# A planned one-core kernel: a table step moved between engines, the PE fillers redistributed, four rows of the combination in four banks

## The chip, the cores and the metric

One core of a Trainium2 chip runs the whole program. The metric is the device time of one execution in microseconds; seven executions of the kernel before have a median of 192.67 us, from 191.19 to 193.7. The profiled execution of the kernel before took 193.35 us, and its trace spans 191.2 us from the first to the last instruction.

The engines carry these names in the profile: PE is the matrix engine (PEld its weight loads), DVE the vector engine, ACT the scalar engine, POOL the GpSimd engine, SP the engine that here only issues transfers. Results of PE go to PSUM, which has eight banks; everything else is in SBUF.

## The reference

Sequence length S is 2048, width D 448, MLP width F 1792, all in bf16. The steps that matter:

```
kv  = (causal 4-tap filter of k with shift_k) * v
y   = irfft(rfft(kv, 2S) * rfft(ssm_k, 2S))[:S] + kv * ssm_D        # a long convolution along S
h   = x + layernorm(x) * y                                          # A_q is x
n   = layernorm(layernorm(h))                                       # the MLP's own norm on top of B's input norm
h2  = h + transpose( gelu( n^T . w1 + b1 ) . w2 + b2 )              # contraction over S, then over F
```

The MLP contracts over the sequence: w1 is 2048 x 1792 and w2 is 1792 x 2048.

## The kernel before

The sequence is split into 16 rows (index r) of 128 positions. A row is a tile of 128 partitions x 448 columns. The convolution is done as a two-stage Fourier transform with matmuls, and the names of the stages are:

- **Tables.** `emit_tables` makes the table `E` of sines (32 matrices of 128 x 128) in two halves, h = 0 for rows 0 to 7 and h = 1 for rows 8 to 15. A half goes through an integer product (L751), an addition (L756), an AND (L759, always DVE) and two sines on ACT (L764). In the kernel before, L751 and L756 of half 0 run on DVE and those of half 1 on POOL. Small index tables follow: counters on POOL, a few fields on DVE up to L745, then L771, L775 and L788 on POOL, which make the second-stage matrix `FW` and the inverse ones.
- **Filler matmuls.** `dummy` (L904) and `emit_warm` (L1047) issue matmuls whose results nobody reads. `N_W0` stand at the start, `N_WK` after each of three groups of transposes of the filter ssm_k, `N_WZ` between the last inverse matmul and the last stage of the convolution, `N_WI` inside that last stage.
- **kT.** `emit_kT` transposes ssm_k with 64 small matmuls (L914) in eight groups of one PSUM bank each; each group is copied out once (L652 on ACT or L655 on DVE, the lines of the helper `evac`).
- **kv.** `emit_kv` first spreads the four taps over the partitions with four matmuls (L868), each copied out as one tap; then, for 8 pairs of rows, two products on DVE (L879), eight matmuls that add them (L885), and one product with v on DVE (L888).
- **k1 and u1.** `emit_stage1` is the first Fourier stage, for the filter (k1) and for kv (u1): per row two matmuls (L933) into a pair of banks, one copy on ACT (L943) into one of eight ring buffers, and two transfers that shuffle partitions (L947), one on POOL's queue and one on SP's. A ring buffer is free again when its two transfers have landed.
- **k2 and u2.** `emit_stage2` (L964) is the second stage, 16 evacuations each (k2 with a scale: L653 on ACT, L656 on DVE; u2: L652, L655). `emit_ct` transposes `E` into `ET`: POOL gathers columns of `E` into four chunks (L985, L990), PE transposes them (L996), one evacuation per chunk.
- **i1.** `emit_products_i1` multiplies the spectra on DVE (L1015), does the first inverse stage on PE (L1027), evacuates, and shuffles with 32 transfers (L1037).
- **i2, the combination.** `emit_i2` runs over rows: two matmuls (L1103), the gate on ACT (L1110), the combination with x on DVE (L1117), a sum of squares on ACT (L1133), four to five tiny steps on POOL (L1140 to L1152, the last a power), and the normed row `Q` on DVE (L1158). Rows 0 and 1 use other statistics (L1123, L1125) and no ACT step. Statistics of x itself come earlier (L1069, L1071 on DVE; L1074, L1077 on POOL). In the kernel before, the two matmuls of any row from 2 on wait for the gate of the row before it.
- **MLP.** `emit_mlp` runs the first seven column groups of w1 row by row as the rows of `Q` come (L1198, 7 matmuls a row into seven banks), the other seven with `Q` complete (L1208), then the second layer (L1218, 224 matmuls) and the sum with h (L1222), whose rows go out as they are done.

The order on each engine is not written by hand. `_Sched` records every operation with a due time (`sch.t0`, set from the constants T_...), an estimated duration (`est`, or a formula in `est_of`), what it reads and writes, and which PSUM bank or ring buffer it needs. `schedule` then plays the operations through on estimated times: at each moment a free engine takes the ready operation with the earliest due time. Operations with `engs=FX` go to ACT or DVE, whichever the plan finds free. What comes out is one fixed list for each engine; on the chip each engine works its list strictly in that order and waits at semaphores. So a changed constant or estimate can move any instruction.

Of the kernel before, what the change touches and what calls it, by code (L numbers as in the profile page):

```python
# [7 lines left out]
ALU = mybir.AluOpType  # L8
# [501 lines left out]
def _build(nc, A_q, A_k, A_v, A_shift_k, A_ssm_k, A_ssm_D, B_w1, B_b1, B_w2, B_b2, out):  # L510
# [55 lines left out]
    with ctx:  # L566
# [72 lines left out]
        T_KV, T_DKV, T_KT, T_K1, T_DK1, T_U1, T_DU1 = -37.75, 0.96, -43.81, -39.56, 0.55, 0.0, 0.9  # L639
        T_K2, T_U2, T_D2, T_CT, T_BIAS, T_I1, T_DI1 = 29.29, 9.62, 1.375, 22.37, 56.3, 12.82, 0.974  # L640
        T_Q, T_DQ, T_I2, T_DI2, T_M1, T_W1 = 83.98, 17.938, 85.76, 0.401, 91.84, 122.45

        T_TH, T_TN = -38.0, -30.0
        T_CP, T_XL, T_WB = 20.0, -37.92, 154.44
        N_WZ, N_WI, N_W0, N_WK = 24, 16, 9, 5
# [15 lines left out]
        def emit_tables():  # L661
# [85 lines left out]
            for h in range(2):  # L747
# [3 lines left out]
                op(("dve", "pool")[h], lambda e, W, h=h, ph=ph: e.tensor_tensor(  # L751
# [4 lines left out]
                op(("dve", "pool")[h], lambda e, W, ph=ph: e.tensor_scalar(  # L756
# [331 lines left out]
        def emit_i2():  # L1088
# [4 lines left out]
            for g, (r0, ng) in enumerate(GR):  # L1093
                oh = o_hst + 64 * g
                hs = view(oh, [16], f32)
                for i in range(ng):
# [5 lines left out]
                    for h in range(2):  # L1102
                        k = op("pe", lambda e, W, b=b, r=r, h=h: e.matmul(  # L1103
                            Pb(b), ET[:, 2 * r + h, :], TZ[:, r, h, :], start=(h == 0), stop=(h == 1)),
                           r=[r_ET(r)] + tz, bw=[b], n=D, after=av[-1:] if r >= 2 and h == 0 else ())
# [8 lines left out]
                    av.append(op(FX, gate, r=[(o_qst + 16 * r, 16), (o_c2, 16)], w=tz, br=[b], n=D, kind="psum"))  # L1114
# [6 lines left out]
                    if ng == 1:  # L1121
                        op("dve", comb, r=rx, w=tz, n=D, est=690.0)
                        op("dve", lambda e, W, hs=hs, A=A: e.bn_stats(out=hs[:, 8:14], in_=A),  # L1123
                           r=tz, w=[(oh + 32, 24)], n=D, kind="1x")
                        op("dve", lambda e, W, hs=hs: e.bn_aggr(out=hs[:, 0:2], in_=hs[:, 8:14]), r=[(oh + 32, 24)],  # L1125
                           w=[(oh, 8)], n=6)
                        mv = [(oh, 4), (oh + 4, 4)]
                        mean, var, rst = hs[:, 0:1], hs[:, 1:2], hs[:, 2:3]
                        o_r = oh + 8
                    else:  # L1130
                        op("dve", lambda e, W, hs=hs, i=i, comb=comb: comb(e, W, acc=hs[:, i:i + 1]), r=rx,
                           w=tz + [(oh + 4 * i, 4)], n=D, est=750.0)
                        op("act", lambda e, W, hs=hs, A=A, i=i: e.activation(out=JK, in_=A, func=ACT.Square,  # L1133
                                                                             scale=1.0 / math.sqrt(D),
                                                                             accum_out=hs[:, 2 + i:3 + i]),
                           r=tz, w=[(oh + 8 + 4 * i, 4), (o_JK, DB)], n=D, est=790.0)
                if ng == 2:
# [4 lines left out]
                       r=[(oh, 8)], w=[(oh + 16, 8)], n=2)  # L1142
                    op("pool", lambda e, W, hs=hs: e.tensor_tensor(out=hs[:, 6:8], in0=hs[:, 4:6], in1=hs[:, 4:6],
                                                                   op=ALU.mult), r=[(oh + 16, 8)], w=[(oh + 24, 8)], n=2)
                    op("pool", lambda e, W, hs=hs: e.tensor_tensor(out=hs[:, 8:10], in0=hs[:, 2:4], in1=hs[:, 6:8],
                                                                   op=ALU.subtract),
                       r=[(oh + 8, 8), (oh + 24, 8)], w=[(oh + 32, 8)], n=2)
# [3 lines left out]
                   r=mv[1:], w=mv[1:], n=2)  # L1151
                op("pool", lambda e, W, var=var, rst=rst, ng=ng: e.tensor_tensor(out=rst, in0=var, in1=cst[:, 0:ng],  # L1152
                                                                                 op=ALU.pow),
                   est=750.0, r=mv[1:] + [(o_c2, 16)], w=[(o_r, 4 * ng)], n=2)
                for i in range(ng):
# [5 lines left out]
                       r=[(o_TZ + r * 2 * DB, 2 * DB), mv[0], (o_r, 4 * ng)], w=[(o_Q + r * DB, DB)], n=D, kind="4x")  # L1161
                if g == 2:
                    emit_warm(N_WI, T_I2 + 0.5, lambda: i2_last[1:2])
# [114 lines left out]
```

## Time and profile before

| what | value |
|---|---|
| profiled execution, time / span | 193.35 us / 191.2 us |
| median of the seven executions | 192.67 us |
| PE busy / DVE / ACT / POOL | 176.6 / 109.9 / 97.5 / 76.9 us |
| first copy of k1 (L943) starts | 14.72 us |
| last product with v (L888) ends | 50.49 us |
| last spectrum product (L1015) ends | 82.17 us |
| last shuffle before the combination lands | 90.21 us |
| first MLP matmul (L1198) starts | 98.14 us |
| MLP without interleaved combination rows starts | 115.45 us |
| last matmul ends | 188.29 us |

Starts and ends are read from the timeline (start, duration, engine, line) and from the chain that ended last. The chain is followed back from the last instruction: at each step to what released it, or to the instruction before it on its engine. PE's busy time holds the fillers too, so a busy PE alone does not say that PE does useful work.

### The profile page before, as it was taken

What the parts mean: (1) busy time and instruction counts of PE and PEld (TensorE: products, weight loads), DVE (VectorE), ACT (ScalarE), POOL (GpSimd) and SP (SyncE); (2) the same over time, 40 slices, a digit from 0 to 9 for tenths busy, and PEclk for the clock granted to TensorE, in tenths of its full rate; (3) what the DMA queues carried; (4) which work ended last, traced back from release to release, by engine and by line L of the source; (5) the groups of instructions that cost most, each with busy time, mean ns of one, the idle gap of its engine ahead of it and who ended that gap; (6) DMA issues with size and microseconds to landing.
All of it is one profiled execution on the core that took longest, in us unless ns stands there. A gap on an engine that the chain in (4) does not pass through costs nothing.

```text
span 191.2 us, 2820 instructions
## 1 busy us (share of the span) xinstructions
PE 176.6 (92%) x1031; PEld 92.3 (48%) x1031; DVE 109.9 (57%) x176; ACT 97.5 (51%) x142; POOL 76.9 (40%) x180
## 2 busy tenths in 40 slices
PE   7949999899988899895989999999999999999993
PEld 2813444234443333242334445555556777777772
DVE  8885679988799999996668975100000222122221
ACT  3477799987989899960489855171221000000000
POOL 8966688679770044468238876000000000000000
PEclk9996699999999999999699999999999999999999
DMA  5997458887539999753899999000000011111111
GB/s 167 418 418 271 143 171 216 233 228 226 173 114 314 393 358 362 233 161 109 282 421 418 418 403 364 8 0 0 0 0 3 8 40 48 48 51 48 48 48 48
DMA packets 15724, 35.43 MB, mean 185 GB/s; under 512 B 3869, under 2 KB 9886, under 8 KB 15710
## 3 DMA queue, kind: packets, MB, share of 16 engines
q1 hardware_dynamic: 11102, 25.59, 35.7%
q0 software_dynamic: 4608, 9.66, 17.0%
q8 instruction: 8, 0.13, 0.3%
q14 instruction: 6, 0.05, 0.1%
HBM read 22.37 MB, written 1.84 MB: 127 GB/s over the span
## 4 chain that ended last, share of the span: by engine, by line
PE 67%; ACT 11%; POOL 7%; DVE 7%; DMA 5%; issue 1%; POOLq 0%
PE ps L1218 22%; PE ps L1208 11%; PE ps L1198 10%; DMA arena<-arena 5%; ACT arena L652 5%; PE ps L1103 4%; PE ps L933 4%; PE ps L1027 4%; PE ps L885 4%; PE ps L964 3%; ACT arena L653 2%; POOL arena L947 2%; ACT arena L1110 2%; POOL arena L756 2%; PE ps L1047 2%
## 5 line engine op out<-in xcount | busy, mean ns | idle before, releaser
L1222 DVE SCALAR_TENSOR_TENSOR arena<-ps,arena 128x448 bf16<-128x448 f32 x16 | 10.9, 684 | 57.9 <-PE ps L1218 57.9
L1218 PE MATMUL ps<-arena 128*128 128x448 bf16 x224 | 42.5, 352 | 0.0
L1218 PEld LDWEIGHTS ps<-arena 128*128 128x128 bf16 x224 | 32.3, 144 | 10.1
L943 ACT CAST arena<-ps 128x896 bf16<-128x896 f32 x32 | 26.9, 926 | 2.5 <-PE ps L933 2.0
L947 POOL DMA_DIRECT2D arena<-arena x32 | 19.3, 603 | 10.3 <-ACT arena L943 7.0
L652 ACT CAST arena<-ps 128x896 bf16<-128x896 f32 (+1 forms) x27 | 22.1, 931 | 1.9 <-PE ps L964 1.1
L1198 PE MATMUL ps<-arena 128*128 128x448 bf16 x112 | 23.0, 352 | 0.0
L1208 PE MATMUL ps<-arena 128*128 128x448 bf16 x112 | 21.4, 352 | 0.0
L933 PE MATMUL ps<-arena 128*128 128x448 bf16 x64 | 17.5, 390 | 3.4 <-ACT arena L652 2.5
L1188 ACT ACTIVATE arena<-ps,arena 128x448 bf16<-128x448 f32 x14 | 8.2, 640 | 20.7 <-PE ps L1208 14.7
L1110 ACT ACTIVATE arena<-ps,arena 128x448 f32<-128x448 f32 x16 | 11.5, 724 | 13.1 <-PE ps L1103 10.7
L879 DVE TENSOR_TENSOR arena<-arena 128x1792 bf16<-128x1792 bf16 x16 | 17.5, 1130 | 0.0
L1037 POOL DMA_DIRECT2D arena<-arena x16 | 9.4, 591 | 19.4 <-DVE arena L655 10.8
L964 PE MATMUL ps<-arena 128*64 128x448 bf16 x128 | 16.0, 360 | 1.0 <-DVE arena L655 0.4
L1015 DVE TENSOR_TENSOR arena<-arena 128x1792 bf16<-128x1792 bf16 x16 | 16.5, 1085 | 0.2 <-ACT arena L653 0.2
L1198 PEld LDWEIGHTS ps<-arena 128*128 128x128 bf16 x112 | 11.0, 98 | 10.2
L1208 PEld LDWEIGHTS ps<-arena 128*128 128x128 bf16 x112 | 11.0, 98 | 10.2
L1027 PE MATMUL ps<-arena 64*128 64x448 bf16 x128 | 14.0, 352 | 1.9 <-ACT arena L652 1.1
L1117 DVE SCALAR_TENSOR_TENSOR arena<-arena 128x448 f32<-128x448 bf16 x16 | 10.8, 685 | 8.0 <-ACT arena L1110 8.0
L885 PE MATMUL ps<-arena 128*128 128x448 bf16 x64 | 14.5, 354 | 0.6 <-ACT arena L943 0.5
L1103 PE MATMUL ps<-arena 128*128 128x448 bf16 x32 | 9.2, 376 | 3.0 <-DMA arena<-arena 2.3
L933 PEld LDWEIGHTS ps<-arena 128*128 128x128 f16 x64 | 5.8, 106 | 12.6 <-ACT arena L652 3.0
(88 smaller groups left out, 205.9 us busy)
## 6 DMA issues: line engine op xcount, KB each, us to landing
arena<-arena POOLq DMA_DIRECT2D x48, 196.0 KB, 4.7
arena<-in_B_w_dram SPq DMA_DIRECT2D x8, 896.0 KB, 14.2
arena<-in_B_w_dram SPq DMA_DIRECT2D x2, 2048.0 KB, 9.9
arena<-in_B_w_dram SPq DMA_DIRECT2D x2, 1536.0 KB, 18.0
arena<-in_A_k_dram SPq DMA_DIRECT2D x4, 448.0 KB, 7.3
arena<-in_A_v_dram SPq DMA_DIRECT2D x4, 448.0 KB, 7.9
arena<-in_A_q_dram SPq DMA_DIRECT2D x4, 448.0 KB, 4.6
out_dram<-arena SPq DMA_DIRECT2D x7, 224.0 KB, 1.9
```

Of the source, the lines that this page charges most:

```text
L652: return e.copy(out=dst(), in_=src())
L879: op("dve", lambda e, W, T=T, i=i, r=r: e.tensor_tensor(out=T[:, i], in0=KH[:, r:r + 4, :], in1=WT, op=ALU.mult), r=[(o_KH + r * DB, 4 * D ...
L885: op("pe", lambda e, W, b=b, T=T, i=i, j=j: e.matmul(Pb(b, i), ID, T[:, i, j, :], start=(j == 0), stop=(j == 3)), r=[(o_ID, 256), (o + (i ...
L933: op("pe", lambda e, W, b=b, r=r, h=h, dl=dl: e.matmul(Pb(b, h), E[:, 2 * r + h, :], src[:, r, :], start=True, stop=not dl), r=[r_E(r), (o ...
L943: return e.copy(out=dst, in_=Ppair(b)) if W == "act" else e.tensor_copy(out=dst, in_=Ppair(b))
L947: shuf[tag + q_ + str(r)] = shuf[tag + q_] = op(q_, lambda e, W, w=w, p0=p0, a=a, b_=b_, j0=j0: e.dma_start(T[p0:p0 + 29:4, j0:j0 + (b_ - ...
L964: op("pe", lambda e, W, b=bs[h], h=h, j=j, c=c, par=par: e.matmul(PS[64 * par:64 * par + 64, b.slots[c], 0:D], FW[:, 64 * c:64 * c + 64], ...
L1027: k = op("pe", lambda e, W, b=bs[h], m=ms[h], par=par, t=t, tab=tab, xy=xy, P=P: e.matmul(Pb(b, par), tab[P, :], MR(m.slots[0])[P, xy, :], ...
L1103: k = op("pe", lambda e, W, b=b, r=r, h=h: e.matmul(Pb(b), ET[:, 2 * r + h, :], TZ[:, r, h, :], start=(h == 0), stop=(h == 1)), r=[r_ET(r) ...
L1198: op("pe", lambda e, W, r=r, fc=fc, b=bs[fc]: e.matmul(Pb(b), W1A[:, r, 128 * fc:128 * fc + 128], Q[:, r, :], start=(r == 0), stop=(r == R ...
L1208: op("pe", lambda e, W, r=r, fc=fc, b=b: e.matmul(Pb(b), W1B[:, r, 128 * (fc - n0):128 * (fc - n0) + 128], Q[:, r, :], start=(r == 0), sto ...
L1218: op("pe", lambda e, W, r=r, fc=fc, b=b: e.matmul(Pb(b), W2[fc // 7][:, fc % 7, r:S:R], G[:, fc, :], start=(fc == 0), stop=(fc == NFC - 1) ...
```

## The change

The diff does five things. Line numbers stay as they are, since each hunk replaces as many lines as it removes.

1. L751 and L756 of table half 1 go from POOL to DVE.
2. Fillers: `N_WK` from 5 to 3 (after each of three transpose groups), `N_WZ` from 24 to 34 (before the combination), `N_WI` from 16 to 6 (inside it; they now follow row 3 instead of row 1).
3. In the combination, the matmuls of rows 0 to 3 wait for no gate; rows 4 and 5 wait for the gates of rows 1 and 2, and only rows from 6 on wait for the row before.
4. Due times of the transposes, k1, u1, u2, i1, the x loads, the statistics of x and the MLP change.
5. Estimates for the combination's operations change (gate 720/620, combination 690, square 570, power 700, other POOL steps 220, norm 510 ns).

```diff
-        T_KV, T_DKV, T_KT, T_K1, T_DK1, T_U1, T_DU1 = -37.75, 0.96, -43.81, -39.56, 0.55, 0.0, 0.9
-        T_K2, T_U2, T_D2, T_CT, T_BIAS, T_I1, T_DI1 = 29.29, 9.62, 1.375, 22.37, 56.3, 12.82, 0.974
-        T_Q, T_DQ, T_I2, T_DI2, T_M1, T_W1 = 83.98, 17.938, 85.76, 0.401, 91.84, 122.45
-        T_TH, T_TN = -38.0, -30.0
-        T_CP, T_XL, T_WB = 20.0, -37.92, 154.44
-        N_WZ, N_WI, N_W0, N_WK = 24, 16, 9, 5
+        T_KV, T_DKV, T_KT, T_K1, T_DK1, T_U1, T_DU1 = -37.75, 0.96, -26.42, -39.56, 0.44, 2.72, 0.9
+        T_K2, T_U2, T_D2, T_CT, T_BIAS, T_I1, T_DI1 = 29.29, -14.6, 1.375, 22.37, 56.3, 7.01, 0.974
+        T_Q, T_DQ, T_I2, T_DI2, T_M1, T_W1 = 83.98, 14.35, 85.76, 0.401, 102.98, 122.45
+        T_TH, T_TN = -36.0, -30.0
+        T_CP, T_XL, T_WB = 20.0, -35.53, 154.44
+        N_WZ, N_WI, N_W0, N_WK = 34, 6, 9, 3
...
-                op(("dve", "pool")[h], lambda e, W, h=h, ph=ph: e.tensor_tensor(
+                op("dve", lambda e, W, h=h, ph=ph: e.tensor_tensor(
...
-                op(("dve", "pool")[h], lambda e, W, ph=ph: e.tensor_scalar(
+                op("dve", lambda e, W, ph=ph: e.tensor_scalar(
...
-                           r=[r_ET(r)] + tz, bw=[b], n=D, after=av[-1:] if r >= 2 and h == 0 else ())
+                           r=[r_ET(r)] + tz, bw=[b], n=D, after=av[r - 3:r - 2] if 3 < r < 6 and h == 0 else av[-1:] if r >= 6 and h == 0 else ())
...
-                    av.append(op(FX, gate, r=[(o_qst + 16 * r, 16), (o_c2, 16)], w=tz, br=[b], n=D, kind="psum"))
+                    av.append(op(FX, gate, r=[(o_qst + 16 * r, 16), (o_c2, 16)], w=tz, br=[b], n=D, est={"act": 720.0, "dve": 620.0}))
...
-                    emit_warm(N_WI, T_I2 + 0.5, lambda: i2_last[1:2])
+                    emit_warm(N_WI, T_I2 + 0.5, lambda: i2_last[3:4])
```

## The prediction

> **What bounds the kernel now.** I read the chain that ended last first, then busy time by stage, then the timeline of each engine inside the stages the change touches. The chain begins with the table's second half:
>
> ```profile
> 1.72 2.60 POOL arena L751
> ...
> 4.53 3.47 POOL arena L756
> ...
> 8.03 2.76 DVE arena L759
> ...
> 10.81 1.79 ACT arena L764
> ...
> 18.44 1.06 PE ps L914 x8
> 19.50 0.75 PE ps L933 x2
> 20.25 1.06 PE ps L914 x8
> ```
>
> The two POOL steps cost 2.60 and 3.47 us; DVE does the same work for half 0 in 1.23 and 0.68 (timeline). The last two transpose groups (L914 x8) stand between rows of k1, so the first four copies L943 start at 14.72, 17.73, 18.55 and 20.28 instead of every 0.82 us.
>
> Then the stages (start:end and length, then busy us and instructions of PE, PEld, DVE, ACT, POOL, then PE clock, DMA share, GB/s):
>
> ```profile
> 14.72:22.20 7.48, 7.48 (x31) 3.18 (x31) 4.30 (x9) 5.11 (x8) 5.76 (x8) 0.57 0.59 200
> 22.20:34.20 12.00, 11.67 (x58) 5.07 (x57) 10.66 (x12) 11.66 (x15) 9.66 (x17) 0.98 0.70 196
> ...
> 58.90:72.00 13.10, 12.08 (x113) 4.66 (x114) 12.97 (x13) 11.93 (x15) 2.34 (x4) 1.00 1.03 379
> 72.00:84.20 12.20, 10.95 (x96) 3.93 (x92) 11.87 (x19) 11.85 (x15) 6.04 (x11) 1.00 0.79 258
> ...
> 90.30:98.10 7.80, 7.43 (x28) 2.77 (x29) 4.76 (x12) 3.92 (x7) 2.40 (x6) 0.78 0.84 308
> ```
>
> From 14.72 to 22.20 DVE is busy 4.30 of 7.48 us. From about 50.4 to 82.17 DVE is full (12.97 of 13.10, 11.87 of 12.20), with ACT close behind: that stage lasts as long as its DVE work. After the last shuffle (it lands at 90.21; I call the moment z) PE sets the end:
>
> ```profile
> 85.05 5.16 DMA arena<-arena
> 90.21 0.05 issue
> 90.26 1.09 PE ps L1103 x4
> 91.35 0.05 issue
> 91.40 2.05 PE ps L1047 x5
> 93.44 0.75 PE ps L1103 x2
> 94.19 0.89 PE ps L1047 x4
> ```
>
> Five fillers take 2.05 us here and four take 0.89: PE runs at half speed until about 94.2 (clock 0.78 over 90.3 to 98.1), after 2.30 us of idleness in front of z. From z to the last matmul at 188.32 are 98.06 us. The 32 + 112 + 112 + 224 = 480 useful matmuls need 0.1892 us each (42.39 / 224 on L1218), 90.8 us together. So 7.2 us are lost after z, 5.2 of them before the first MLP matmul at 98.14: 7.88 us less seven combination rows of 2 x 0.19.
>
> **The change, part 1: the front.** DVE's new list is L751, L756 of half 0, the identities, L759, then L751, L756, L759 of half 1. From 1.34: 1.2 + 0.3 + 0.7 + 0.2 + 1.2, then 1.2 + 0.7 + 0.15 + 1.2 = 6.9 us, so half 1 is ready at 8.2. Bounds: L759 took 1.21 once and 2.75 beside POOL's counters, and the two small identity steps took 1.92 and 1.03 beside POOL's table work; with both L759 at 2.75 and one such stall of 0.3 the end is 11.6. I take 8.8, nearer to 8.2, because POOL's long instructions are gone from this stretch. Before: 10.78.
>
> The gain does not go to k1. All 16 remaining transposes, the four L868 and the first L996 group now stand before it on PE, and the L868 pass through one free bank after another: about 5.1 us after half 1, so k1 starts at 13.9 (before 13.44) and L943 at 15.2. What goes is the stutter behind it: the fifth L943 starts at 15.2 + 4 x 0.82 = 18.5 instead of 22.09. The ring takes part back: the ninth and later copies wait for shuffle transfers that POOL first issues at about 16.2 (its L771 need L745 on DVE, at 14.1), with 4.8 us to landing; k1 ends some 1.6 to 2.4 us earlier.
>
> DVE gains more. Its taps and transposed groups no longer wait for PE (before: 1.92 + 0.17 + 0.87 + 1.18 us idle between 13.8 and 21.4). Its three L879 in a row began at 22.17; now they can begin when L777 is done, whose input POOL's L775 delivers at 18.1: 18.5. The halo of k, issued at 7.3 and 7.8 with 10.3 and 10.0 us to landing, allows 17.8. So the kv products are 3.7 us ahead. They need 15 x 1.09 + 8 x 1.09 + waits for L885 as before (3.6), since banks still come from ACT; the last L888 ends near 46.9 instead of 50.49.
>
> Part 1 continued, to z. DVE then has 13 evacuations of 1.086 and 16 products of 1.085: 31.5 us, against 31.7 before (12 evacuations, one L655 of ET, one L1069). The u shuffles land about 54, when DVE has used up its six k2 evacuations (46.9 + 6.5 = 53.4), so I add 1.3 us of waiting. The last L1015 ends at 79.7, 2.5 us earlier. ACT has the same 35 evacuations and ET copies after its last L943 and is no later. One thing goes against it: L1077 (0.74) and both L1069 pairs now stand before POOL's last two L1037. They end 2.5 us after the last L1015, the last evacuation 2.0 after it; cost 0.4. **z comes 2.1 us earlier** (bounds: 0 if the u shuffles land no sooner, 3.8 if nothing waits: 46.9 + 31.5 = 78.4 against 82.17).
>
> **Part 2: fillers and the combination.** 34 fillers of 0.196 last 6.7 us; from the last inverse matmul at 83.15 to z were 7.1. They fill the gap without reaching z, so PE meets z at full clock (bounds: they overrun by 0.4 if z comes that much nearer; left half-clocked, the start costs 1 us more). Fewer `N_WK` fillers: six of 0.19 to 0.37, all beside waits for half 1; nothing.
>
> From z on: rows 0 to 3 take 8 x 0.19 = 1.5 us, six fillers to 2.65, rows 4 and 5 to 3.4 (their gates, rows 1 and 2, end at 1.9 and 2.6), row 6 at 4.6 behind the gate of row 5 (ACT: first gate at 0.59 as before, six at 0.62 to 0.72). The first normed row is a chain of latencies: gate 0.72, two combinations to 2.6, statistics to 3.95 (2.58 from the first combination, as before), POOL 0.46 + 0.72 to 5.2, L1158 at 5.4 to 5.85. So the first L1198 starts at z + 5.9 instead of 7.88, with the same seven rows of the combination done. Loss 5.9 - 2.65 = 3.25 against 5.2. Before, 10 more fillers and the half clock stood in the place; what is late next is Q itself.
>
> Afterwards each row from 7 on waits some 0.05 us for its gate, a few times: 0.25. The old losses there were 2.0. Walking ACT, DVE and POOL behind it (1.37 us per row, as the gate loop now at 98 to 107 shows), the tightest places are the gate of row 10, due at 16.1 where PE needs it at 16.6, and the last normed row at 28.3 where PE comes at 28.6, after three L1208 moved in. So loss 3.5 instead of 7.2: **3.7 us** (bounds 1.6 if every gate is late by 0.2, 4.2).
>
> **Sum:** 193.35 - 2.1 - 3.7 = 187.55, say 187.5. The profiled execution lies 0.7 above the median; the same step from the median gives 186.9. What lies outside the span (2.15 us) I leave.
>
> [...] L985 shows the row: the same POOL copy takes 0.37 to 1.28 us, 1.28 at 43.26 beside an L879. L759 on DVE took 1.21 inside POOL's 3.47 us L756, so there DVE was not held to the end. [...]
>
> **Rivals.**
>
> *Front gain lost before z (0.18).* DVE is ahead, but the u shuffles land at 56.7 as now, because POOL's list of 32 L947 at 0.81 plus copies sets them. Against it: POOL idled 7.0 us for L943, and seven L985 and three L771 move ahead of the loop's bulk. Only part 2 remains: 193.35 - 3.7 + 0.4 = 190.0.
>
> *The new order after z doesn't start the MLP earlier (0.10).* If Q row 0 still comes at z + 7.9, only the later losses (about 1.7) go: 193.35 - 2.1 - 1.7 = 189.5.
>
> *Slower: POOL's table copies (0.10).* Nine copies (six for L996, three more) now stand before the first L947 on POOL and, through L996, before k1. At the worst row, 1.28 each, with three L771 at 1.19: 9.3 + 11.5 + 3.6 = 24.4 for the first L947 (before 15.93). Then 31 x 0.81, ten copies (10.5) and L775, L788, L791 (3): last issue at 63.8 instead of 53.7. 193.35 + 10.1 - 3.7 = 199.7; half that delay gives 194.7. It decides from a mean copy of about 0.9 us: 9.3 + 8.1 + 2.1 + 0.9 + 25.1 + 9 + 3 = 57.5, which eats part 2.
>
> **How the numbers follow.** My forecast has 0.62. Low end, both upper bounds taken from the median: 192.67 - 3.8 - 4.2 = 184.7. High end: past the first two rivals, 190.6. One per cent, about what a measurement of this kernel can tell from no change, is 1.9 us. Faster: 0.62 + most of the first two rivals, 0.80; same 0.10; slower 0.10.
>
> **What would show it.** Right: L759 of half 1 ends before 10 us; L933 and L943 run at 0.82 from the first on; the L879 triple starts near 18.5; last L1015 near 80; no half-clock slice at z; first L1198 6 us after z. Wrong: POOL copies near 1.3 us before the first L947, or L1198 waiting for Q at rows 2 to 4.

## The result, and the profile after

| | before | after |
|---|---|---|
| median of all executions | 193.33 us (64) | 191.53 us (27) |
| lowest to highest | 190.59 to 195.12 | 189.04 to 193.41 |
| profiled execution, time / span | 193.35 / 191.2 us | 192.2 / 190.4 us |
| time outside the span, median of the executions | 2.20 us (2.13 to 2.31) | 1.82 us (1.76 to 1.88) |
| granted clock, mean of the profiled execution | 0.973 | 0.982 |
| z (PE starts the first L1103) | 90.26 | 90.31 |
| first MLP matmul, L1198 | 98.14 (z + 7.88) | 96.70 (z + 6.39) |
| from z to the end of the last L1218 | 98.02 | 97.17 |

The ratio is 0.9936, 95% interval 0.9908 to 0.9964. The change makes the kernel faster by 0.6%. The forecast was 187.5 us with a range of 184.7 to 190.6, and 191.53 lies outside it. The ratio leaves out executions more than 1.5% above the fastest of the same kernel, so it lies nearer to one than the quotient of the medians (0.991).

**The front.** The chain that ended last, in the kernel after (start, us, engine, buffer, line):

```profile
12.96 1.82 PE ps L914 x16
14.78 0.85 PE ps L996 x8
15.63 0.37 PE ps L933
16.00 0.48 PE ps L937
...
17.49 0.91 ACT arena L943
...
23.85 6.49 DMA arena<-arena
...
30.90 6.75 DMA arena<-arena
```

The table is gone from the chain; PE's transposes have taken its place. But PE needs 0.48 us for one L937, which took 0.29 before: it runs at half rate (the trace's clock records have 0.50 from 13.76 to 20.59), and k1 comes 2.0 us later than before. In PE's timeline its first matmul starts at 15.43 against 13.44; the chain lays its pieces end to end and has 15.63. The two shuffles on the chain take 6.49 and 6.75 us to land. The stages, same windows as before up to z, the last one from after's own z (columns as above: busy us of PE, PEld, DVE, ACT, POOL, clock, DMA share, GB/s):

```profile
14.72:22.20 7.48, 7.28 (x29) 2.66 (x27) 4.86 (x13) 4.55 (x6) 4.78 (x8) 0.61 0.57 196
22.20:34.20 12.00, 10.80 (x54) 4.71 (x52) 11.44 (x12) 11.43 (x15) 9.47 (x18) 1.00 0.79 220
58.90:72.00 13.10, 11.80 (x106) 4.73 (x104) 12.73 (x13) 12.00 (x15) 1.41 (x3) 1.00 1.04 390
72.00:84.20 12.20, 10.82 (x96) 3.85 (x97) 11.86 (x16) 11.70 (x15) 6.92 (x13) 1.00 0.78 222
90.30:98.10 7.80, 5.71 (x28) 2.41 (x28) 5.67 (x15) 6.37 (x12) 3.44 (x7) 1.00 0.83 303
```

The clock is 0.61 in the first window, much as the 0.57 before. Behind z it is 1.00 instead of 0.78: that part of the change works. Until z nothing is won: the last L1015 ends at 82.54 (82.17 before).

**After z.** PE's timeline (start, us, line, shape, count, idle time ahead and what ended it):

```profile
90.31 1.69 PE L1103 MATMUL ps<-arena 128*128 128x448 bf16 x8
92.05 1.31 PE L1047 MATMUL ps<-arena 128*128 128x448 f16 x6
...
96.70 0.36 PE L1198 MATMUL ps<-arena 128*128 128x448 bf16 x1 [0.97 <-DVE arena L1158]
...
101.39 6.22 PE L1198 MATMUL ps<-arena 128*128 128x448 bf16 x32
109.51 0.55 PE L1103 MATMUL ps<-arena 128*128 128x448 bf16 x2 [1.90 <-ACT arena L1110]
```

Four rows of the combination run in one go at 0.19 us a matmul, as intended. Besides 1.06 us for the gate of row 5, for which the forecast had 1.2, there are two waits: 0.97 us for the first normed row, and 1.90 us ahead of the matmuls of row 11, which wait for the gate of row 10, the tightest place of the forecast. The chain says what that gate waited for:

```profile
105.10 0.94 DVE arena L1158 x2
106.04 0.09 DVE arena L1071
106.13 1.05 DVE arena L1069 x2
...
107.24 0.51 POOL arena L1074
...
107.83 0.87 POOL arena L1077
...
108.73 0.73 ACT arena L1110
...
109.51 0.55 PE ps L1103 x2
```

The statistics of x of that row (L1071 on DVE, L1074 and L1077 on POOL) stand behind normed rows on DVE. Their due time is `T_Q + T_DQ * g` with g = 5, and DVE's list puts the L1071 of rows 10 and 11 behind normed rows, at 104.14 and 105.95. POOL's list has L1074 behind the steps of a row as well; the power that ends them ran from 106.45 to 107.16.

### The profile page after: what moved, and what is told of

Read it like the earlier page. It is cut to its first block, busy times and chain, and to the rows that moved or that the text cites. A ratio compares the mean times of both kernels' runs of the same rounds, so it can differ in the third digit from the quotient of the medians.

```text
span 190.4 us, 2810 instructions
## 1 busy us (share of the span) xinstructions
PE 175.2 (92%) x1025; PEld 92.5 (49%) x1025; DVE 110.2 (58%) x179; ACT 97.6 (51%) x141; POOL 72.8 (38%) x178
## 4 chain that ended last, share of the span: by engine, by line
PE 63%; POOL 10%; DMA 9%; DVE 7%; ACT 7%; issue 3%; POOLq 0%; ACTq 0%
PE ps L1218 22%; PE ps L1208 11%; DMA arena<-arena 9%; PE ps L1198 6%; PE ps L1027 5%; ACT arena L652 4%; PE ps L964 3%; PE ps L914 3%; PE ps L904 3%; PE ps L885 2%; POOL arena L947 2%; POOL arena L1152 2%; PE ps L933 2%; ACT arena L943 2%; PE ps L1103 1%
## 5 line engine op out<-in xcount | busy, mean ns | idle before, releaser
L1218 PE MATMUL ps<-arena 128*128 128x448 bf16 x224 | 42.5, 352 | 0.0
L1218 PEld LDWEIGHTS ps<-arena 128*128 128x128 bf16 x224 | 32.3, 144 | 10.1
L943 ACT CAST arena<-ps 128x896 bf16<-128x896 f32 x32 | 26.9, 922 | 5.5 <-PE ps L937 2.8
L1198 PE MATMUL ps<-arena 128*128 128x448 bf16 x112 | 23.0, 353 | 1.0 <-DVE arena L1158 1.0
L947 POOL DMA_DIRECT2D arena<-arena x32 | 19.2, 601 | 10.0 <-ACT arena L943 6.7
L1208 PE MATMUL ps<-arena 128*128 128x448 bf16 x112 | 21.5, 352 | 0.0
L879 DVE TENSOR_TENSOR arena<-arena 128x1792 bf16<-128x1792 bf16 x16 | 18.2, 1176 | 0.0
L933 PE MATMUL ps<-arena 128*128 128x448 bf16 x64 | 17.6, 387 | 0.4 <-ACT arena L943 0.2
L1037 POOL DMA_DIRECT2D arena<-arena x16 | 9.4, 593 | 20.8 <-PE ps L964 15.6
L885 PE MATMUL ps<-arena 128*128 128x448 bf16 x64 | 14.5, 354 | 2.7 <-ACT arena L943 2.2
L1198 PEld LDWEIGHTS ps<-arena 128*128 128x128 bf16 x112 | 10.9, 98 | 11.7 <-DVE arena L1158 2.0
L1015 DVE TENSOR_TENSOR arena<-arena 128x1792 bf16<-128x1792 bf16 x16 | 16.4, 1086 | 0.0
L1117 DVE SCALAR_TENSOR_TENSOR arena<-arena 128x448 f32<-128x448 bf16 x16 | 10.5, 681 | 4.7 <-ACT arena L1110 4.6
L655 DVE CAST arena<-ps 128x896 bf16<-128x896 f32 (+2 forms) x11 | 9.5, 877 | 2.7 <-PE ps L868 1.2
L964 PEld LDWEIGHTS ps<-arena 128*64 128x64 f16 x128 | 5.4, 108 | 11.4 <-ACT arena L652 4.6
```

What stands on the lines that cost most here:

```text
L879: op("dve", lambda e, W, T=T, i=i, r=r: e.tensor_tensor(out=T[:, i], in0=KH[:, r:r + 4, :], in1=WT, op=ALU.mult), r=[(o_KH + r * DB, 4 * D ...
L885: op("pe", lambda e, W, b=b, T=T, i=i, j=j: e.matmul(Pb(b, i), ID, T[:, i, j, :], start=(j == 0), stop=(j == 3)), r=[(o_ID, 256), (o + (i ...
L933: op("pe", lambda e, W, b=b, r=r, h=h, dl=dl: e.matmul(Pb(b, h), E[:, 2 * r + h, :], src[:, r, :], start=True, stop=not dl), r=[r_E(r), (o ...
L943: return e.copy(out=dst, in_=Ppair(b)) if W == "act" else e.tensor_copy(out=dst, in_=Ppair(b))
L947: shuf[tag + q_ + str(r)] = shuf[tag + q_] = op(q_, lambda e, W, w=w, p0=p0, a=a, b_=b_, j0=j0: e.dma_start(T[p0:p0 + 29:4, j0:j0 + (b_ - ...
L964: op("pe", lambda e, W, b=bs[h], h=h, j=j, c=c, par=par: e.matmul(PS[64 * par:64 * par + 64, b.slots[c], 0:D], FW[:, 64 * c:64 * c + 64], ...
```

## The experiments

Two questions came out of this. Why is z no earlier, although the instructions of the front stand in the order that was expected? And what is the new order after z worth by itself? Mean clocks and medians by clock below are over all executions of a kernel, so that executions of equal clock are compared.

### The change cut in two

`front_only` has the table on DVE (L751 and L756), `N_WK`, and the lines of due times that start with T_KV, T_K2, T_TH and T_CP from the change; the combination, its estimates and its fillers stay as before.

```diff
-        N_WZ, N_WI, N_W0, N_WK = 24, 16, 9, 5
+        N_WZ, N_WI, N_W0, N_WK = 24, 16, 9, 3
...
-                op(("dve", "pool")[h], lambda e, W, h=h, ph=ph: e.tensor_tensor(
+                op("dve", lambda e, W, h=h, ph=ph: e.tensor_tensor(
...
```

> The front of the change alone: the table's second half on DVE, N_WK 3 and the changed due times; fillers, gate waits and estimates of the combination stay as before. Theory (the front brings nothing by the last shuffle, because k1 starts 2 us later and the lead of the kv products melts): z within 0.5 us of 90.2, time within 0.5% of the kernel before. Rival (the front does bring 2 us, and the combination part spoils them): z near 88.1, ratio near 0.989.

Measured: median 191.25 us, ratio 0.9889 (0.9834 to 0.9944). Its z is at 90.58, with 2.10 us of idleness ahead of it, yet at full clock; its first L1198 comes at z + 6.48 and its last matmul 96.86 us behind z. So the front alone gives all that the whole change gives, and its profile shows none of it ahead of z.

`comb_only` is the other part: the kernel after with those same lines as in the kernel before.

```diff
-                op("dve", lambda e, W, h=h, ph=ph: e.tensor_tensor(
+                op(("dve", "pool")[h], lambda e, W, h=h, ph=ph: e.tensor_tensor(
...
-        N_WZ, N_WI, N_W0, N_WK = 34, 6, 9, 3
+        N_WZ, N_WI, N_W0, N_WK = 34, 6, 9, 5
```

> The combination part alone (34 and 6 fillers, the gate waits, the estimates, T_DQ 14.35, T_M1 102.98) on the kernel before's front. Theory (all of the measured gain is here): first L1198 about 6.4 us after z instead of 7.88, a wait of 1.5 to 2 us for the gate of a row near 10, ratio near 0.994, as the whole change. Rival (the gain is the front's): ratio 1.000 or more.

Measured: 192.37 us, ratio 0.9998 (0.9958 to 1.0039). z 90.42, 96.87 from there to the end, where before's profile had 98.02. The combination's new order does not show in the times.

`after_again` is the kernel after, unchanged.

> The changed kernel once more, beside the others. Theory: k1's first copy again near 17.5, z near 90.3, a wait of about 2 us for the gate of row 10. Rival (the profile of after showed an unusual execution): first copy near 15.2 and z 1 us or more earlier, no wait at row 10.

Measured: 191.13 us, ratio 0.9927 (0.9877 to 0.9977), and this time the profiled execution ran at a granted clock of 1.00 throughout. Its chain:

```profile
12.32 1.53 PE ps L914 x16
13.85 0.45 PE ps L996 x8
14.30 0.19 PE ps L933
14.49 0.29 PE ps L937
...
15.40 0.91 ACT arena L943
```

The same instructions now start k1 at 14.30 instead of 15.63, and z is at 88.53 instead of 90.31. The forecast had 13.9 and 88.1. The forecast's front is nearly there, in an execution whose granted clock shows no half rate; the question becomes what the kernel before does in such an execution.

`table_half` moves L751 and L756 of half 1 to DVE and leaves every constant as before.

```diff
-                op(("dve", "pool")[h], lambda e, W, h=h, ph=ph: e.tensor_tensor(
+                op("dve", lambda e, W, h=h, ph=ph: e.tensor_tensor(
...
-                op(("dve", "pool")[h], lambda e, W, ph=ph: e.tensor_scalar(
+                op("dve", lambda e, W, ph=ph: e.tensor_scalar(
```

> The kernel before with L751 and L756 of half 1 on DVE and nothing else changed; the planner makes a new order from the old due times. Theory (the move pays only together with due times that fit it): half 1 ready before 9 us as in the changed kernel, but u2, i1 and the combination come in another order, and z is 90 or later: ratio 1.000 to 1.025. Rival (the move alone is the front's gain): z near 88, ratio near 0.989.

Measured: 193.8 us, ratio 1.0071 (1.0029 to 1.0113). k1 starts at 10.73, 2.7 us earlier than before, and the last L943 ends at 50.37 (52.85 before), but z is at 93.43, 3.2 us later. With the old due times the plan mixes second-stage and inverse work so that DVE waits 4.5 us in total for one kind of result, where before it waited 0.4 (us in total, times, longest):

```profile
DVE arena L655 <- PE ps L964: 4.5, 4, 2.5
```

In this plan an early front is worth nothing, because the due times behind it were not made anew.

### The half-clocked stretches

Up to the last matmul, the time at a granted clock of 0.50 comes in multiples of 3.41 us: 6.83 us in the front and 3.41 behind z in before's, 6.83 in after's, 10.24 in one of the runs below (`stats`, clock 0.973), none in others (`after_again`, clock 1.00). So the two profiles compared in the result stand in different clocks.

`fill_gap` is the kernel before with ten more fillers ahead of the combination (their estimate is set so that the plan does not move).

```diff
-        N_WZ, N_WI, N_W0, N_WK = 24, 16, 9, 5
+        N_WZ, N_WI, N_W0, N_WK = 34, 16, 9, 5
```

> The kernel before with ten more fillers in front of the combination (34 instead of 24) and nothing else moved. Theory (the 7.88 us from z to the first L1198 were 6.5 us of latency and 1.4 us of half clock): the clock is 1.00 after z, first L1198 at z + 6.5; the time falls by up to 1.4 us, by less in the median if not every execution had the half clock there: ratio 0.993 to 1.000. Rival (the order of fillers and gates makes the 7.88 us, as the prediction had it): first L1198 still at z + 7.5 or later.

Measured: 191.98 us, ratio 0.9966 (0.9927 to 1.0005). PE's timeline behind z, with the old order:

```profile
90.29 0.93 PE L1103 MATMUL ps<-arena 128*128 128x448 bf16 x4 [0.49 <-DMA arena<-arena]
91.28 1.12 PE L1047 MATMUL ps<-arena 128*128 128x448 f16 x5
...
96.77 0.73 PE L1198 MATMUL ps<-arena 128*128 128x448 bf16 x3
```

The same five fillers take 1.12 us that took 2.05, and the first L1198 comes at z + 6.48 instead of 7.88. So 1.4 us of the 7.88 were the half clock, and the old order, at full clock, needs 96.63 us from z to the end. The new order needed 97.17, 0.5 us more. Part of that goes with the new front ahead of it: behind the old front (`comb_only`) the new order needs 96.87, 0.2 us more.

`warm_before` is the kernel before with twelve more fillers in the 2.53 us in which PE waits for the table's second half; no other instruction moves.

```diff
-                        dummy(N_WK, T_KT + 0.9 * g, (k,))
+                        dummy(N_WK, T_KT + 0.9 * g, (k,), 12 * (i == 2))
...
-                op("pe", lambda e, W: e.matmul(Pb(dumb), DUM[:, 0:128], DUM, start=True, stop=True),
+                op("pe", lambda e, W, m=more * (i == 0): [e.matmul(Pb(dumb), DUM[:, 0:128], DUM, start=True, stop=True) for _ in range(m + 1)][-1],
```

> The kernel before with twelve more fillers in the 2.53 us in which PE waits for table half 1 (10.91 to 13.44); nothing else moved. Theory (that idle stretch sets off the half-clocked stretch from 15.8 to 22.7, and fewer half-clocked stretches are a part of what the change gains): mean clock of the executions up from 0.98 to 0.99 or more, time 1 to 2 us less, ratio 0.990 to 0.995. Rival (the half clock comes whatever PE does there): same clocks, ratio 1.000, or 1.002 if the fillers overrun.

Measured: 191.27 us, ratio 0.995 (0.9905 to 0.9996). The mean clock rises from 0.978 to 0.994. First PE's timeline of the kernel before, then that of `warm_before`:

```profile
9.23 1.68 PE L904 MATMUL ps<-arena 128*128 128x448 bf16 x8
13.44 0.36 PE L933 MATMUL ps<-arena 128*128 128x448 bf16 x1 [2.53 <-ACT arena L652]
```

```profile
9.62 3.95 PE L904 MATMUL ps<-arena 128*128 128x448 bf16 x20
13.44 0.36 PE L933 MATMUL ps<-arena 128*128 128x448 bf16 x1
```

k1 starts at the same 13.44 in both. Nothing became earlier, no work moved, and the kernel is about as much faster as with the whole change (0.9936). `warm_fill` has both sets of fillers, and its profiled execution ran at full clock:

```diff
-        N_WZ, N_WI, N_W0, N_WK = 24, 16, 9, 5
+        N_WZ, N_WI, N_W0, N_WK = 34, 16, 9, 5
...
-                        dummy(N_WK, T_KT + 0.9 * g, (k,))
+                        dummy(N_WK, T_KT + 0.9 * g, (k,), 12 * (i == 2))
```

> The kernel before with both groups of fillers (twelve while PE waits for table half 1, ten in front of the combination) and nothing else moved. Theory (a large part of the measured gain of the change is a higher mean clock, which fillers give without moving anything): mean clock 0.99 or more, from z to the last matmul 96.6 us, median 190.5 to 191.5, ratio 0.988 to 0.994, as the whole change. Rival (the two do not add): ratio 0.995, as with the twelve alone.

Measured: 190.85 us, ratio 0.9895 (0.9842 to 0.9948). This is the old order, every instruction in its old place, at a clock of 1.00: z at 88.81, 96.63 from there to the end. The kernel after at full clock has 88.53 and 97.16.

The z of the profiles by the half-clocked stretches ahead of z (kernels whose front has other work or another order are left out: `table_half`, and `warm_front` and `warm_stats` below):

| stretches ahead of z | old front | new front |
|---|---|---|
| none | 88.81 (`warm_fill`) | 88.53, 88.65, 88.22, 89.39 (`after_again`, `front_fill`, `stats_again`, `row0_first`) |
| one | 89.66, 89.83 (`warm_before`, `warm_comb`) | |
| two | 90.26, 90.29, 90.42 (before, `fill_gap`, `comb_only`) | 90.31, 90.58 (after, `front_only`) |
| three | | 90.32 (`stats`) |

Where a line has both, old and new lie within 0.6 us, in both directions. Behind the old front one stretch costs 0.85 and 1.02 us at z and two cost 1.45 to 1.61, and the new front gains nothing there that these profiles can tell from their spread.

`front_fill` puts the ten fillers of `fill_gap` into `front_only`:

```diff
-        N_WZ, N_WI, N_W0, N_WK = 24, 16, 9, 3
+        N_WZ, N_WI, N_W0, N_WK = 34, 16, 9, 3
```

> The front of the change with the old combination and 34 fillers in front of it: against the changed kernel, the old order of gates and fillers after z, nothing else. Theory (at full clock the new order is 0.5 us worse than the old one, since it saves 0.1 us to the first L1198 and loses 2 us at row 10): first L1198 at z + 6.5, last matmul at z + 96.6 against 97.2, ratio 0.987 to 0.991. Rival (the new order is the better one): last matmul at z + 97.2 or later, ratio 0.993 or more.

Measured: 190.3 us, ratio 0.9883 (0.9824 to 0.9943), 96.86 from z to the end. New front and old combination at full clock: `after_again` with its new combination needs 97.16. The old order after z is 0.2 to 0.5 us the better one: 0.3 by this pair, 0.2 behind the old front (`comb_only` against `fill_gap`), 0.5 by `warm_fill` and `after_again`.

The executions at a granted clock of 1.00 show a gain that the profiles do not. The new front with the old combination (`front_only` and `front_fill`: 9 executions, median 189.76 us) is 0.9 us below the old front with it (`warm_before` and `warm_fill`: 10, 190.66) and 0.75 below the whole change (`after` and `after_again`: 16, 190.51). Of the 0.9, 0.4 lie outside the span. So at equal clock the new front is worth about half a microsecond inside the span, in executions of one kernel that lie 0.6 to 4 us apart, and the new combination takes about as much away. (These ran on three chips; at a clock of 0.99 the kernel before has 191.34 to 191.45 on each.)

### The late statistics

`stats` makes the statistics of x of rows up to 11 due early:

```diff
-                sch.t0 = T_Q + T_DQ * g
+                sch.t0 = min(T_Q + T_DQ * g, T_Q + 1.0) if g < 6 else T_Q + T_DQ * g
```

> The changed kernel with the statistics of x for rows 0 to 11 all due before the combination, so that the two aggregates of rows 10 and 11 stand right behind their own statistics instead of behind six normed rows. Theory (row 10's gate is late only because its aggregate stands in the wrong place of DVE's list): the wait of 2 us in front of row 10 or 11 goes, 2.0 us less than the changed kernel, ratio about 0.984. Rival (POOL's steps of 0.5 us pace everything, so the wait returns at a later gate or normed row): 0.5 us less or nothing, ratio 0.991 to 0.994.

Measured: 189.63 us, ratio 0.9857 (0.9787 to 0.9928). From z to the end 95.95 instead of 97.17. DVE does the L1071 pair of rows 10 and 11 at 89.78, ahead of z, instead of at 104.14 and 105.95; PE:

```profile
101.34 1.12 PE L1198 MATMUL ps<-arena 128*128 128x448 bf16 x5 [0.78 <-DVE arena L1158]
...
105.42 7.16 PE L1198 MATMUL ps<-arena 128*128 128x448 bf16 x37
112.60 0.55 PE L1103 MATMUL ps<-arena 128*128 128x448 bf16 x2
```

The 37 matmuls run straight into the next combination row: the wait of 1.90 us is gone, and 0.78 us of it comes back earlier, where PE now waits for a normed row. `stats_again` repeats it.

> The changed kernel with early statistics once more, beside the other on the same chip. Theory: ratio 0.984 to 0.988, executions of equal mean clock up to 2 us apart, since PE sets the front here and its first half-clocked stretch varies. Rival: 1% below the kernel with the old front.

Measured: 189.76 us, ratio 0.9868 (0.9809 to 0.9926), z 88.22 at full clock, 95.96 from z to the end. This one edit makes a version faster than both kernels.

`row0_first` goes on from `stats`: DVE does combination, statistics and aggregate of row 0 in one go, ahead of row 1. The edit takes away the latency that the plan adds behind an instruction, for L1117 and L1123 of these two rows.

```diff
-                        op("dve", comb, r=rx, w=tz, n=D, est=690.0)
+                        sch.ops[op("dve", comb, r=rx, w=tz, n=D, est=690.0)].lat = 0.0
...
-                           r=tz, w=[(oh + 32, 24)], n=D, kind="1x")
+                           r=tz, w=[(oh + 32, 24)], n=D, kind="1x")].lat = 0.0
```

> The kernel with early statistics, and the combination, statistics and aggregate of row 0 in a row on DVE ahead of row 1's. Theory (what is left of the 6.4 us from z to the first L1198 is a chain of latencies through DVE and POOL, not fillers): first L1198 about 1.2 us earlier, at z + 5.2, and the time 0.5 to 1.2 us less than with early statistics alone, ratio 0.980 to 0.983. Rival (rows behind it come late in exchange): first L1198 earlier, but waits of the same size at rows 1 to 4, ratio 0.986.

Measured: 190.13 us, ratio 0.9857 (0.9777 to 0.9936). Its PE timeline, z being 89.39:

```profile
94.64 1.11 PE L1198 MATMUL ps<-arena 128*128 128x448 bf16 x5
...
99.73 0.55 PE L1103 MATMUL ps<-arena 128*128 128x448 bf16 x2 [0.82 <-ACT arena L1110]
```

The first L1198 comes at z + 5.25 instead of 6.63, and the end only 0.31 us sooner (95.64): the gate of row 9 is late in its place. What comes after z is a pipeline of ACT, DVE and POOL at 1.37 us a row, and a start that is earlier by itself waits for it later.

### Is the front bound by PE now?

`warm_front` puts four more fillers behind each of the four L868 of the kernel after.

```diff
-                op("pe", lambda e, W, b=b, j=j: e.matmul(
+                op("pe", lambda e, W, b=b, j=j: [e.matmul(
...
+                    [e.matmul(Pb(dumb), DUM[:, 0:128], DUM, start=True, stop=True) for _ in range(4)]][0],
```

> The changed kernel with four fillers behind each of the four L868, sixteen in all, in the stretch from 9 to 13 us in which PE is full of transposes and one-row matmuls. Theory (this work does not keep the clock up, 128-row matmuls do): mean clock of the executions up from 0.990 to 0.995 or more; k1 starts up to 1.5 us later at full clock than 14.3, and the time stays within 0.5 us of the changed kernel's, ratio 0.991 to 0.996. Rival (the half clock there has nothing to do with what PE runs): clocks as before, time 1 to 2 us more, ratio 0.998 to 1.004.

Measured: 193.52 us, ratio 1.0094 (1.0051 to 1.0138). The mean clock rises from 0.990 to 0.996, and the kernel is 2 us slower than the kernel after (median against median): sixteen fillers of 0.19 are 3.0 us, and they delay k1. The first L943 starts at 20.73 in its profile, z is at 93.29. The waits for half 1 in which the fillers of the kernel before cost nothing are no longer there. `warm_stats` is `warm_front` with the early statistics.

```diff
-                sch.t0 = T_Q + T_DQ * g
+                sch.t0 = min(T_Q + T_DQ * g, T_Q + 1.0) if g < 6 else T_Q + T_DQ * g
```

> The same sixteen fillers in the kernel with early statistics. Theory: as early statistics alone with less spread, ratio 0.982 to 0.987. Rival (the fillers only delay k1): 1 us or more above early statistics alone, ratio 0.991 or more.

Measured: 192.29 us, ratio 0.9966 (0.9925 to 1.0007); 95.97 from z to the end. The early statistics bring 1.2 us here too (median against median; 193.25 against 192.06 at a clock of 1.00). The two have the same front, instruction for instruction, and both profiles show a granted clock of 1.00 from end to end. Yet first `warm_front` and then `warm_stats` on PE (their line numbers are one higher: L905 are fillers, L915 transposes):

```profile
8.22 1.48 PE L915 MATMUL ps<-arena 128*128 128x128 bf16 x12
9.50 1.28 PE L905 MATMUL ps<-arena 128*128 128x448 bf16 x3
```

```profile
7.16 0.91 PE L915 MATMUL ps<-arena 128*128 128x128 bf16 x12
7.91 0.73 PE L905 MATMUL ps<-arena 128*128 128x448 bf16 x3
```

Three fillers take 1.28 us in the one and 0.73 in the other. In its first microseconds PE runs at about half rate: the first nine fillers of before and of after take 3.54 us, 0.39 each, where eight take 1.68 from 9.23 on in before. The end of that differs from execution to execution: the 24 transposes from 4.85 on take 2.83 us in `warm_front` and 2.09 in `warm_stats`, the two fillers behind them 0.95 and 0.54, and only from the first L868 on (0.55 in both) are the two alike. The clock column does not show it: the trace's clock records open with the first full-rate stretch, at 5.58 us in before and at 6.93 in after, and the column counts what lies ahead of it as full. In a front bound by PE it moves everything: the first L943 is at 20.73 and 18.58. That fits the wider spread of the kernel after at one clock: at 1.00 it lies between 189.41 and 193.41. It is, by estimate, also a part of what sets its two profiles apart: of the 1.33 us by which after's k1 is later in the chain than that of `after_again`, 0.64 are there when the last 16 transposes start (12.96 against 12.32), ahead of the stretch that begins at 13.76, where the clock column shows no half rate in either.

### The new combination without the new front

`warm_comb` is `comb_only` with the fillers of `warm_before` and the early statistics: if the clock is all that the front brings, it should be as fast as `stats`.

```diff
-                        dummy(N_WK, T_KT + 0.9 * g, (k,))
+                        dummy(N_WK, T_KT + 0.9 * g, (k,), 12 * (i == 2))
...
-                sch.t0 = T_Q + T_DQ * g
+                sch.t0 = min(T_Q + T_DQ * g, T_Q + 1.0) if g < 6 else T_Q + T_DQ * g
```

> The front of the kernel before (table half 1 on POOL, its due times) with the twelve fillers while PE waits, the combination part of the change, and the statistics of x for rows 0 to 11 due before the combination. Theory (at an equal clock the new front brings 0.3 us at most): z 88.8 to 89.7, last matmul at z + 96.0, ratio 0.982 to 0.987, within 0.3% of stats_again. Rival (the new front is worth 2 us at an equal clock): ratio 0.992 or more, 1% above stats_again.

Measured: 191.55 us, ratio 0.9929 (0.9891 to 0.9968), in the same runs as the 0.9868 of `stats_again`; at a clock of 1.00 it is 190.95 against 189.25 for the two `stats` runs. So it is slower by 1.2 us (by the ratios) to 1.8 us (by the medians), and the clock is not all. One part stands in its PE timeline:

```profile
104.92 5.46 PE L1198 MATMUL ps<-arena 128*128 128x448 bf16 x28
111.40 0.55 PE L1103 MATMUL ps<-arena 128*128 128x448 bf16 x2 [1.03 <-ACT arena L1110]
```

In its plan a later gate is late, and from z to the end are 96.90 us instead of 95.96: 0.94. Outside the span it has 2.2 us instead of 1.82: 0.4. What is left, up to 0.5, is within the spread of z. So a front that is earlier by 2.6 us at DVE is worth half a microsecond or less at z, but the plan that came with it lets the early statistics work.

## Why the prediction was wrong

Term by term, profile against profile: the front was to bring 2.1 us up to z and lost 0.05; the order after z was to bring 3.7 and brought 0.85 (1.4 by the clock, which ten more fillers alone bring in `fill_gap`, less 0.5 by the order); outside the span nothing was forecast and some 0.4 came.

**The base of the front.** The step that failed: "z comes 2.1 us earlier", and in it "What goes is the stutter behind it: the fifth L943 starts at 15.2 + 4 x 0.82 = 18.5 instead of 22.09", with DVE's idle times between 13.8 and 21.4 taken as waits of the order. Both were read from a trace that ran at half rate from 15.8 to 22.7, which its clock of 0.57 in that window said, and the forecast of the new front was made at full rate. So the clock's loss was booked as the order's: 2.0 of the 3.6 us of stutter, and 1.6 of DVE's 4.1 us of waiting for PE (in `warm_fill` 1.93 + 0.17 + 0.44 us of it are still there). The timelines of ACT, first the old order at full clock (`warm_fill`), then the new one (`after_again`):

```profile
14.71 0.91 ACT L943 CAST arena<-ps 128x896 bf16<-128x896 f32 x1 [0.53 <-PE ps L937]
...
17.35 1.71 ACT L943 CAST arena<-ps 128x896 bf16<-128x896 f32 x2
19.36 6.65 ACT L943 CAST arena<-ps 128x896 bf16<-128x896 f32 x8
```

```profile
15.40 8.19 ACT L943 CAST arena<-ps 128x896 bf16<-128x896 f32 x10 [1.38 <-PE ps L937]
```

The old order's fifth copy, the second of the eight, starts at 20.1, not 22.09. Step by step:

| step | forecast | after, profile | after at full clock | old order at full clock |
|---|---|---|---|---|
| L759 of half 1 ends | 8.8 | 8.53 | | |
| k1 starts (PE's timeline) | 13.9 | 15.43 | 14.13 | 13.43 |
| first L943 | 15.2 | 17.49 | 15.40 | 14.71 |
| fifth L943 | 18.5 | 21.0 | 18.6 | 20.1 |
| L879 triple | 18.5 | 20.90 | 18.82 | 21.40 |
| last L888 ends | 46.9 | 50.05 | 48.44 | 48.92 |
| last L1015 ends | 79.7 | 82.54 | 80.93 | 80.59 |
| z | 88.1 | 90.31 | 88.53 | 88.81 |

At full clock the forecast's new front holds within half a microsecond down to the triple and again at z; it is the old one that stands 1.45 us earlier than the trace it was subtracted from. By these two profiles, the 2.16 us from 90.26 to the forecast's 88.1 are 1.45 of clock, 0.43 by which the new front is later than forecast, and 0.28 that the order gains. In between the forecast was 1.5 and 1.2 us too early (last L888, last L1015); that it fits again at z is luck, as the next paragraph shows.

**Within the front** a second step was off: "waits for L885 as before (3.6)" (with it the terms add up to 47.2, not 46.9). The triple comes 2.6 us ahead of the old order at equal clock (18.82 against 21.40), but the last L888 only 0.5. DVE now waits 4.2 us for L885 against 2.6 in `warm_fill`. The lead is spent before the kv products end. The cost of 0.4 for POOL's steps ahead of the last L1037 did come, as 0.3: its transfer starts 3.17 us after the end of the last L1015 in after and `after_again`, and 2.89 us after it in before and `warm_fill`. After's chain has the step:

```profile
84.35 0.72 POOL arena L1077
85.07 0.64 POOL arena L1037
85.71 4.55 DMA arena<-arena
```

What hides the cost is the transfer behind it, which landed after 4.55 and 4.38 us in the new order and after 5.16 and 5.28 in the old one. So from the last L1015 to z are 7.6 us in `after_again` and 8.2 in `warm_fill`, where the forecast had 8.4. Why the transfer was shorter is open.

**What the clock is worth.** The chance that an execution has fewer half-clocked stretches was no term of the sum, and by the estimate below it is most of the gain. All executions, by granted clock, median us (number):

| clock | before (98) | after and `after_again` (40) |
|---|---|---|
| 1.00 | none | 190.51 (16) |
| 0.99 | 191.37 (23) | 191.13 (12) |
| 0.98 | 192.19 (22) | 191.88 (4) |
| 0.97 | 193.56 (38) | 192.02 (8) |
| 0.965 | 194.80 (15) | none |

Weighted by their numbers, these medians average 192.93 and 191.13, 1.8 us apart. With the kernel after's shares of the clocks, the kernel before would have 0.4 x 190.5 (three executions of `warm_fill`; the seven of `warm_before` have 190.72) + 0.3 x 191.37 + 0.1 x 192.19 + 0.2 x 193.56 = 191.5. So, as an estimate, about 1.4 us come from the clock and 0.4 from what is left, the size of what came outside the span (0.38). Kernels in which PE idles 2.3 to 2.5 us ahead of k1 have a mean clock of 0.978 to 0.982 (before, `comb_only`, `fill_gap`); those in which it does not, 0.988 to 0.997 (all others). The change's part in this is that the transposes, and not fillers, now fill that gap.

**After z.** "Loss 5.9 - 2.65 = 3.25 against 5.2": the 5.2 held 1.4 us of half clock, which the fillers alone take away (`fill_gap`). At full clock the old order's first L1198 comes 6.48 us after z and the new order's 6.39, so the reordering gained 0.1 there. The half microsecond to the forecast's 5.9 is POOL: the two L1149 of rows 0 and 1 run ahead of the first power and take 0.67 and 0.54 where 0.46 stood for both.

"The gate of row 10, due at 16.1 where PE needs it at 16.6": right place, wrong time. The gate started at z + 18.4 and PE waited 1.90 us for it. The walk assumed that statistics and normed rows share DVE in the order of need; DVE's fixed list has L1071 behind two normed rows. `stats` shows it by taking it away: 1.2 us of the 1.90. POOL's tiny steps, 0.22 in the plan, cost 0.47 to 0.54 for the first rows (L1140, L1143, L1145, L1149). So the loss after z was 97.17 - 90.8 = 6.4 us instead of 3.5: 3.7 up to the first L1198, 1.9 at the gate, the rest small gaps.

**Outside the span.** "What lies outside the span (2.15 us) I leave": it fell by 0.38 us. Every kernel with L751 and L756 of half 1 on POOL has 2.18 to 2.21 on average, every one with them on DVE 1.81 to 1.90. `table_half`, in which nothing else was edited, has 1.83, so the move is enough for it. Why is open.

**What held.** The table's half 1 (8.53 against 8.8), the order on PE, the filled gap ahead of z (clock 1.00 there, rows 0 to 3 in 1.69 us), row 10 as the tightest place. L759 of half 1 took 1.23 us with POOL at work beside it, and POOL's copies L985 took 0.40 us in the median, one of them 1.26, so the slower rival with its table copies at 1.28 each did not come (its terms add up to 63.0, not 63.8). Not all went without a stall: L756 of half 0 took 1.39 us on DVE, where it had taken 0.68.

**The rivals.** The outcome is that of "front gain lost before z", but not by its mechanism. POOL's list does not set the u shuffles; POOL waits for ACT:

```profile
L947 POOL DMA_DIRECT2D arena<-arena x32 | 19.2, 601 | 10.0 <-ACT arena L943 6.7
```

That is after's group of L947 (busy us, mean ns, then idle us and what ended them). "The new order after z doesn't start the MLP earlier" is right at equal clock (6.39 against 6.48).

**The gap that halves the rate.** Where a trace has half-clocked time ahead of its last matmul, it is 3.41, 6.83 or 10.24 us. In the two traces of the result every change of rate lies a whole number of times 3.413 us behind the first full-rate record: 3, 5, 25 and 26 times in before (from 5.58), 2 and 4 times in after (from 6.93). With a gap of 2.53 us in the front the kernel before was below full clock in every one of 98 executions (7 of 12 were at full clock once it was filled, and none of the 24 of `comb_only` and `fill_gap`, which keep the gap), and with 2.30 us ahead of z it fell to half rate in its profiled one, at 90.91. 2.10 and 2.52 us there (`front_only`, `warm_before`) did not do it. So the length of a gap alone does not decide. In the kernel before the 2.30 us, from 87.96 to 90.26, lie between two such multiples, 87.50 and 90.91, and the rate falls at the second. In `warm_before`, whose rate falls at about 16.9 (its four L933 from 16.77 on take 1.57 us, 0.93 in `warm_fill`), 21 steps of 3.413 us further on are at about 88.6 and cut the gap, from 87.14 to 89.66, in two. That ahead of z a gap of this size decides by where it falls is an estimate from these two profiles; no run moved a gap.

A gap is not needed either. The kernel after fell to half rate at 13.76, and in the 3.41 us before that its PE had no gap: 1.1 us of transposes, 1.4 of one-row matmuls (three L868 of 0.48) and 0.9 of fillers. Nor are transposes needed: `warm_before` fell to half rate at about 16.9, and in the 3.41 us before that its PE had neither a gap nor a transpose.

```profile
13.73 0.36 PE L937 MATMUL ps<-arena 1*128 1x448 bf16 x1
...
15.10 1.74 PE L868 MATMUL ps<-arena 1*128 1x448 bf16 x4
16.77 1.57 PE L933 MATMUL ps<-arena 128*128 128x448 bf16 x4
```

One-row matmuls, two L937 and four L868, fill about 2.2 of these 3.41 us. In the kernel before, 1.0 us of the gap and the first of the same one-row matmuls lie in the 3.41 us from 12.41 to 15.82, at whose end the rate falls. What transposes add, no run here shows.

## What to carry to other kernels

Before a trace is used as the base of a sum, look at its granted clock: a stage that ran at half rate must be brought to full rate, or the new order be costed at half rate too, or the clock's loss is counted as a gain of the edit. Then ask what fills PE's idle times, for here twelve fillers in a gap of 2.53 us were worth about as much as the whole reordering (ratio 0.995 against 0.9936), until PE itself was the bound; there sixteen fillers, 3.0 us of work, made the kernel 2.0 us slower. And where a planner writes fixed lists, the small operation that is due late (two aggregates and two POOL steps here) is what a tight gate will wait for: look for it on the list, not in the sum of busy times.

## What was not expected of the hardware

- The granted clock of a profile does not show PE's slow first microseconds: the same three matmuls took 1.28 and 0.73 us at a clock of 1.00, and k1 moved by 2.1 us with them.
- In 98 executions the kernel before never ran at full clock; twelve idle-time matmuls brought 7 of 12 executions there.
- Two POOL instructions on 1024 integers a partition, moved to DVE, took 0.38 us from the time outside the span.
- A shuffle of 196 KB from POOL's queue landed in 4.55 to 6.75 us on the chain of one execution.
